# Cutting 12,160 tokens into 384 and 23 times 512, and loading a weight by one DMA for each 32 partitions

## The chip, the core and the metric

The kernel runs on one core of a Trainium2 chip. Its time is device time in microseconds (us) for one execution. Three runs of the kernel before took 2182.74, 2184.99 and 2193.29 us; the median, 2184.99 us, is the time before. The profile comes from one more execution, which took 2181.22 us. Its span, from the first instruction to the end of the last, is 2179.4 us; 1.8 us lie around it.

The engines are named as in the profile: PE multiplies matrices, DVE and ACT work on vectors, SP issues DMAs, and PEld is PE loading a stationary operand.

## The reference

Three stages over two sequences of 6080 tokens of width 256, in float32:

```
f = lower_bound + (1 - lower_bound) * sigmoid(f_logit);  h = f*h + (1-f)*x   # a scan over the tokens
y1 = relu(h @ w_in1)**2 @ w_out1                                             # 256 -> 2048 -> 256
y2 = elu(y1 @ w_in2) @ w_out2                                                # 256 -> 2048 -> 256
```

## The kernel before

**Tiling.** The 12,160 tokens are cut into blocks (`block_sizes`): one of 256, then 22 of 512, a rest of 384, and one of 256, 25 blocks in all. A slot is one block, one of the two layers (`m` = 0 or 1) and one of eight groups of 256 of the 2048 inner features. For each slot PE first makes the group's inner features in PSUM ("first" and "later"), ACT and DVE evict them and apply the activation, and PE then adds the group's share of the output to accumulators ("out"). After the eighth group ACT copies the accumulators out: layer 0 goes through DRAM and comes back as the input of layer 1, layer 1 goes to the result.

**Precision.** Each operand is held as a high and a low part of 32-bit numbers, and a product is three matmuls. All matmuls have a stationary operand of 128 x 128; what differs is the number of columns that move past it.

**Matmuls of a slot, for a block of n tokens.** The input product cuts the block into two halves and the features into two, and makes the four products of that 2 x 2 scheme by seven block products: 21 matmuls of n/2 columns (line 600). The first four blocks of layer 0 (`PLAIN = 4`) use eight block products instead, laid out as 12 matmuls of n columns (line 614). The output product of layer 0 is 12 matmuls of n columns (line 699, written as acc<-g,wo), that of layer 1 is 6n/128 matmuls of 256 columns (line 699, acc<-wo,g).

**Order over blocks.** Blocks are taken in pairs. A run is one layer over one pair, its slots woven together, the pair's second block starting two slots after its first. The runs are layer 0 of pairs 0 and 1, then in turn layer 1 of a pair and layer 0 of the pair two further on, and at the end layer 1 of the last two pairs. With 25 blocks the thirteenth pair holds one block, the last of 256 tokens, alone. Layer 1 of blocks 2 and 3 is the first run in which every block has 512 tokens and both layers' weights are made.

**Weights.** In the first run each of the eight groups of layer 0's input weights is loaded (`add_weights`, its step `load`), turned into its high and low part by two instructions of ACT (lines 371, 374) and four of DVE or ACT (377, 380, 397 or 399, 403), and stored to DRAM. Later runs stream the groups back in from DRAM (line 460), once for each run. `load_w` issues the load. For layer 0's input weights it is two DMAs on SP's queue, one for each half k of the 256 rows (line 320): each fills all 128 partitions, and its rows in DRAM are ordered as 4 groups q of 32 partitions i. Output weights are one DMA (line 313), layer 1's input weights one DMA (line 316).

**The scan.** `add_scan` loads half a block of `f_logit` and of `x` by four DMAs each (line 533, one for each 32 partitions), transposes them, applies the gate, and scans. The tiles `fs` and `xs` have one buffer each, so a half's loads wait until the half before has been transposed (line 542). `add_parts` then makes the high and low parts of the block, which PE reads (lines 492, 494, 500).

**What sets the order.** Every piece of work is a step with an engine, a cost and a due time. `Order.run` goes through the steps with these costs and writes out one list, by earliest due time among what is ready; each engine executes its part of the list in order. Before that list come a dummy activation of ACT (line 864), two DMAs of `lower_bound` on SP's queue (line 866), and two DVE instructions that make `ga` and `gb` from it (867, 868).

Of the kernel before, what the change touches and what calls it, by code (L numbers as in the profile page):

```python
# [11 lines left out]
AF = mybir.ActivationFunctionType  # L12
ALU = mybir.AluOpType
# [2 lines left out]
P = 128  # L16
TB = 512
HB = 256
FIRST = (256,)
LAST = (256,)  # L20
LEAD = 2
PLAIN = 4
BEHIND = 2
# [14 lines left out]
def block_sizes(total):  # L38

    ends = sum(FIRST) + sum(LAST)  # L40
    mid = [TB] * ((total - ends) // TB)
    rest = total - ends - sum(mid)
    return [*FIRST, *mid, *([rest] if rest else []), *LAST]

# [110 lines left out]
def kernel(  # L155
# [11 lines left out]
    nc = tc.nc  # L167
# [3 lines left out]
    KD = D // P  # L171
# [15 lines left out]
    lb = const.tile([P, KD], F32, name="lb")  # L187
    ga = const.tile([P, KD], F32, name="ga")
    gb = const.tile([P, KD], F32, name="gb")
    carry = const.tile([P, KD], F32, name="carry")  # L190
    warm = const.tile([P, 1], F32, name="warm")
# [41 lines left out]
    def new(tag, shape, dtype=F32, name=None):  # L233
        return pools[tag].tile(shape, dtype, tag=name or tag, name=name or tag)
# [29 lines left out]
    for i, s in enumerate(slots + [None] * (LAG + 1)):  # L264
        n = sizes[s[1]] if s else 0
        if s:
            if s[0] == 1 and s[2] == 0:
                while any(p[:2] == (0, s[1]) for _, p, _ in pending):
                    _, p, _ = pending.pop(0)
# [6 lines left out]
        while pending and (not s or i - pending[0][0] >= LAG or now - pending[0][2] >= AGE * sizes[pending[0][1][1]] / TB):  # L276
            _, p, _ = pending.pop(0)
# [9 lines left out]
    order = Order()  # L287

    def act(n, psum=False):
        return (0.05 if psum else 0.09) + n / 1172  # L290

    def dve(n, fast=False):
        return 0.067 + n / (1920 if fast else 960)

    def chain(due, steps):

        left = sum(st[1] + order.SLACK for st in steps)
        for e, us, what, *rest in steps:
            order.add(e, us, due - left, what, *rest)
            left -= us + order.SLACK  # L300
# [4 lines left out]
    CF = 256  # L305
    CE = 512
    ws_t = {}

    def load_w(st, m, kind, c):
        w = ((w_in1, w_out1), (w_in2, w_out2))[m][kind].bitcast(I32)  # L310
        if kind == 1:
            v = w[c * CF : (c + 1) * CF, :].rearrange("(k p) u -> p k u", p=P)
            nc.sync.dma_start(st.rearrange("p k e w -> p k (e w)"), v)
        elif m == 1:
            v = w[:, 2 * c * CF : 2 * (c + 1) * CF].rearrange("(k p) u -> p k u", p=P)
            nc.sync.dma_start(st.rearrange("p k e w -> p k (e w)"), v)
        else:
            v = w[:, 2 * c * CF : 2 * (c + 1) * CF].rearrange("(q k i) u -> k q i u", q=4, k=KD)
            for k in range(KD):
                nc.sync.dma_start(st[:, k].rearrange("p e w -> p (e w)"), v[k])  # L320

    n_a = {"a": 0, "wp": 0}

    def key_of(tag):
        n_a[tag] += 1
        return tag, n_a[tag] - 1
# [31 lines left out]
    def add_weights(i, m, kind, c, due, wk=None):  # L358
        t = {}

        def load(e):
            t["st"] = new("st", [P, 2, CE // 2, 2], I32)
            load_w(t["st"], m, kind, c)
            sv = t["st"].rearrange("p k e w -> p (k e) w")
            t["low"], t["high"] = sv[:, :, 0], sv[:, :, 1]

# [41 lines left out]
        def keep_whole(e):  # L408
            nc.sync.dma_start(rd[c], t["a"])

        st, a = ("st", i), key_of("a")
        steps = [
            ["SP", 0.95 if m == 0 and kind == 0 else 0.475, load, (), [st], None, 512],
            ["ACT", act(CE), scaled, [st], [a]],
            ["ACT", act(CE), low_bits, (), [st]],
            ["DVE", dve(CE), magnitude, [st], [a]],
            ["DVE", dve(CE), sign, [st], [a]],
        ]
        if m == 1 and kind == 0:
            q = key_of("a")  # L420
            chain(due - 6.0, [*steps, ["DVE", 4 * dve(P), sums, [a], [q]]])
            add_kept_parts(t, "a", a, m, c, 0, due - 2.0)
            add_kept_parts(t, "q", q, m, c, 4, due)
            return
        w = ("ws", wk) if kind == 0 else ("w", m, c)
# [96 lines left out]
    def add_scan(i, b, h, due):  # L522
        n = sizes[b] // 2
        t0 = starts[b] + h * n
        u = n_unit[0, b]
        t = {}
# [16 lines left out]
            return go  # L543

        def gate(e):
            f = t["fT"]
            for c in range(KD):
                nc.vector.tensor_scalar(f[:, c], f[:, c], ga[:, c : c + 1], gb[:, c : c + 1], op0=ALU.mult, op1=ALU.add)  # L548
# [274 lines left out]
    for due, what, m, g, s in weights:  # L823
        if what == "load":
            add_stream(m, s[1], g, due, n_ws)
        elif what == "sums":
            add_sums(g, due)
        else:
            add_weights(n_prep, m, int(what == "out"), g, due, n_ws)
            n_prep += 1  # L830
        if s:
            use[s] = n_ws
            n_ws += 1
# [6 lines left out]
    for kind, s in pe_order:  # L840
        m, b, g = s
# [19 lines left out]

    with tc.manual_schedule():
        nc.vector.memset(warm, 0.0)
        nc.scalar.activation(warm, warm, AF.Exp)
        for c in range(KD):
            nc.sync.dma_start(lb[:, c : c + 1], lower_bound.rearrange("(q c i o) -> c q i o", q=4, c=KD, o=1)[c])
        nc.vector.tensor_scalar(ga, lb, -0.5, 0.5, op0=ALU.mult, op1=ALU.add)
        nc.vector.tensor_scalar(gb, lb, 0.5, 0.5, op0=ALU.mult, op1=ALU.add)
        order.run()


# [23 lines left out]
```

## Time and profile before

| | us |
|---|---|
| time, median of 3 runs | 2184.99 |
| the profiled execution's own time | 2181.22 |
| its span | 2179.4 |
| PE busy | 2085.8 (96% of the span), 15072 matmuls |
| PE loading stationary operands | 1968.1 (90%) |
| DVE busy | 1729.9 (79%) |
| ACT busy | 1712.1 (79%) |
| mean granted clock of PE | 0.997 |
| DMA | 282.84 MB, 130 GB/s in the mean |

The share of busy time is a mean over stages with different limits. A matmul's busy time overlaps with that of the next one, since they are pipelined; what one matmul costs is read from the time between the starts of two neighbouring rows of the timeline, divided by the number of matmuls. A stretch of PE is read from where a run's first matmul starts: 25.8 us for the first of all, 379.4 us for layer 1 of blocks 2 and 3, and from there on one layer-1 run and one layer-0 run at a time.

### The profile page before, as it was taken

The numbers are of one execution on the slowest core, as the hardware profiler recorded it, in microseconds if no ns is written. First come the engines' busy times: TensorE is split into PE (matmuls) and PEld (weight loads), VectorE is DVE, ScalarE is ACT, GpSimd is POOL, SyncE is SP. The second block draws the span as 40 slices with busy tenths as digits, with TensorE's granted clock in tenths as the row PEclk, the third lists the DMA queues.
The fourth block names the chain that finished last, engine by engine and source line by source line (L and its number), as shares of the span: only waits on it lengthen the run. The fifth ranks groups of instructions, "written<-read, shape, count | busy, mean of one in ns | idle before, by whom it ended". The sixth has DMA issues, their size and how long they took to land.

```text
span 2179.4 us, 38016 instructions
## 1 busy us (share of the span) xinstructions
PE 2085.8 (96%) x15072; PEld 1968.1 (90%) x15072; DVE 1729.9 (79%) x2938; ACT 1712.1 (79%) x2243; POOL 0.2 (0%) x4
## 2 busy tenths in 40 slices
PE   2999899999999999999999999999999999999998
PEld 1877889999999899899899899999999989999998
DVE  5787896986985986987887798798698598677675
ACT  3786787887887887888888888788788788778675
POOL 0000000000000000000000000000000000000000
PEclk9999999999999999999999999999999999999999
DMA  5777643432542442433433433343253243233524
GB/s 154 218 236 241 194 157 108 120 124 94 135 130 95 130 130 92 133 101 119 120 109 124 126 102 124 113 115 126 100 136 122 95 123 127 87 112 106 185 85 141
DMA packets 213049, 282.84 MB, mean 130 GB/s; under 512 B 111112, under 2 KB 137608, under 8 KB 212872
## 3 DMA queue, kind: packets, MB, share of 16 engines
q1 hardware_dynamic: 212872, 280.42, 41.2%
q8 instruction: 119, 1.95, 0.4%
q14 instruction: 58, 0.48, 0.1%
HBM read 236.59 MB, written 43.78 MB: 129 GB/s over the span
## 4 chain that ended last, share of the span: by engine, by line
PE 68%; DVE 19%; ACT 6%; DMA 4%; issue 2%; SPq 1%; DVEq 0%; ACTq 0%
PE acc L699 35%; PE pc L600 31%; DVE g L672 4%; DVE r L643 2%; DVE F L565 2%; PE pc L614 1%; DVE r L662 1%; DVE s L631 1%; ACT s L628 1%; DVE r L639 1%; DMA ws<-wd 1%; DVE s L636 1%; DMA xs<-in_x_dram 1%; DVE fT L548 1%; DVE xA L500 1%
## 5 line engine op out<-in xcount | busy, mean ns | idle before, releaser
L699 PE MATMUL acc<-wo,g 128*128 128x256 f32 x4560 | 585.1, 283 | 17.8 <-DVE g L672 16.7
L699 PEld LDWEIGHTS acc<-wo,g 128*128 128x128 f32 x4560 | 561.3, 189 | 23.2 <-DVE g L672 21.4
L699 PE MATMUL acc<-g,wo 128*128 128x512 f32 (+2 forms) x2400 | 555.9, 382 | 2.1 <-DVE wo L403 2.1
L600 PE MATMUL pc<-xB,ws 128*128 128x256 f32 (+2 forms) x3864 | 507.6, 281 | 11.7 <-ACT s L628 11.2
L600 PE MATMUL pc<-xA,ws 128*128 128x256 f32 (+2 forms) x3864 | 506.3, 280 | 12.9 <-ACT s L628 12.9
L600 PEld LDWEIGHTS pc<-xA,ws 128*128 128x128 f32 x3864 | 481.6, 189 | 24.2 <-ACT s L628 18.5
L672 DVE TENSOR_TENSOR g<-r,g 128x1024 fp32r<-128x1024 f32 (+2 forms) x400 | 465.6, 1164 | 45.0 <-ACT g L667 43.9
L600 PEld LDWEIGHTS pc<-xB,ws 128*128 128x128 f32 x3864 | 482.5, 189 | 20.4 <-ACT s L628 13.7
L699 PEld LDWEIGHTS acc<-g,wo 128*128 128x128 f32 x2400 | 427.8, 189 | 78.0 <-DVE wo L403 2.3
L667 ACT ACTIVATE g<-r 128x1024 fp32r<-128x1024 f32 (+2 forms) x400 | 406.3, 1016 | 58.0 <-DVE r L662 50.6
L636 DVE TENSOR_TENSOR s<-pc,s 128x256 f32<-128x256 f32 (+2 forms) x368 | 150.5, 409 | 286.8 <-PE pc L600 286.1
L628 ACT ACTIVATE s<-pc 128x768 f32<-128x768 f32 (+2 forms) x368 | 286.9, 780 | 62.4 <-PE pc L600 61.1
L643 DVE TENSOR_TENSOR r<-pc,s 128x512 f32<-128x512 f32 (+2 forms) x368 | 244.3, 664 | 11.3 <-ACT r L646 5.9
L662 DVE SCALAR_TENSOR_TENSOR r<-e,r 128x1024 f32<-128x1024 f32 (+1 forms) x200 | 232.3, 1162 | 25.2 <-ACT e L659 25.2
L646 ACT ACTIVATE r<-pc 128x256 f32<-128x256 f32 (+2 forms) x368 | 137.0, 372 | 139.2 <-DVE r L643 87.1
L656 ACT ACTIVATE e<-r 128x1024 f32<-128x1024 f32 (+1 forms) x200 | 202.8, 1014 | 19.3 <-DVE r L639 14.9
L649 ACT ACTIVATE r<-r 128x768 f32<-128x768 f32 (+2 forms) x168 | 138.5, 824 | 97.8 <-DVE r L639 97.7
L652 ACT ACTIVATE r<-r 128x1024 f32<-128x1024 f32 (+1 forms) x200 | 203.6, 1019 | 5.7
L659 ACT ACTIVATE e<-e 128x1024 f32<-128x1024 f32 (+1 forms) x200 | 203.2, 1016 | 5.1
L631 DVE TENSOR_TENSOR s<-s 128x256 f32<-128x256 f32 (+2 forms) x368 | 150.1, 408 | 16.8 <-ACT s L628 9.4
L639 DVE TENSOR_TENSOR r<-s 128x256 f32<-128x256 f32 (+2 forms) x368 | 149.5, 406 | 0.0
L614 PE MATMUL pc<-xA,ws 128*128 128x256 f32 (+1 forms) x192 | 41.0, 368 | 29.0 <-DVE xA L494 25.8
(49 smaller groups left out, 858.0 us busy)
## 6 DMA issues: line engine op xcount, KB each, us to landing
ws<-wd SPq DMA_DIRECT2D x192, 896.0 KB
out_dram<-o SPq DMA_DIRECT2D x47, 256.0 KB
fs<-in_f_logit_dram SPq DMA_DIRECT2D x176, 64.0 KB
xs<-in_x_dram SPq DMA_DIRECT2D x176, 64.0 KB
xd<-o SPq DMA_DIRECT2D x44, 256.0 KB
F<-xd SPq DMA_DIRECT2D x44, 256.0 KB
st<-in_moe_w_out_dram SPq DMA_DIRECT2D x16, 512.0 KB
wd<-wp SPq DMA_DIRECT2D x24, 256.0 KB
```

What stands on the lines that cost most here:

```text
L600: nc.tensor.matmul(t["pc"][:, c], lhsT=ws[:, p, w], rhs=x_t[m, b][:, r, v], start=(which is FIRST_PRODUCTS and q == 0 and c in (1, 2)), st ...
L628: nc.scalar.activation(t["s"], t["pc"][:, 1:4], AF.Copy)
L631: nc.vector.tensor_tensor(t["s"][:, 1], t["s"][:, 1], t["s"][:, 2], op=ALU.add)
L636: nc.vector.tensor_tensor(t["s"][:, 0], t["pc"][:, 0], t["s"][:, 0], op=ALU.add)
L643: nc.vector.tensor_tensor(t["c"][:, 1:3], t["pc"][:, 2:4], u, op=ALU.add)
L652: nc.scalar.activation(t["r"], t["r"], AF.Square)
L656: nc.scalar.activation(t["e"], t["r"], AF.Relu, scale=-1.0)
L659: nc.scalar.activation(t["e"], t["e"], AF.Exp, scale=-1.0)
L662: nc.vector.scalar_tensor_tensor(t["r"], t["e"], 1.0, t["r"], op0=ALU.subtract, op1=ALU.max)
L667: nc.scalar.activation(t["g"][:, 0], t["r"], AF.Copy)
L672: nc.vector.tensor_tensor(t["g"][:, 1], t["r"], t["g"][:, 0].bitcast(F32), op=ALU.subtract)
L699: nc.tensor.matmul(a, lhsT=u, rhs=v, start=clear and k == 0, stop=two and k == 2, skip_group_check=True)
```

## The change

Five edits. `FIRST` and `LAST` make the blocks 384 and 23 times 512: 24 blocks, twelve full pairs. `load_w` takes the queue as an argument, and layer 0's input weights are loaded by four DMAs, one for each 32 partitions, each of them with both halves k; the step's cost in the plan goes from 0.95 to 1.9. The first of these loads is issued on ACT's queue, and its step is put ahead of all others (due -20, cost 0.1 on SP). Behind it on ACT's queue come the two DMAs of `lower_bound`, and then the dummy activation. `ga` and `gb` are made in the first `gate`.

```diff
-FIRST = (256,)
-LAST = (256,)
+FIRST = (384,)
+LAST = ()
...
-    def load_w(st, m, kind, c):
+    def load_w(queue, st, m, kind, c):
...
-            nc.sync.dma_start(st.rearrange("p k e w -> p k (e w)"), v)
+            queue.dma_start(st.rearrange("p k e w -> p k (e w)"), v)
...
-            v = w[:, 2 * c * CF : 2 * (c + 1) * CF].rearrange("(q k i) u -> k q i u", q=4, k=KD)
-            for k in range(KD):
-                nc.sync.dma_start(st[:, k].rearrange("p e w -> p (e w)"), v[k])
+            v = w[:, 2 * c * CF : 2 * (c + 1) * CF].rearrange("(q k i) u -> q i k u", q=4, k=KD)
+            for q in range(4):
+                queue.dma_start(st[32 * q : 32 * q + 32].rearrange("p k e w -> p k (e w)"), v[q])
...
-            load_w(t["st"], m, kind, c)
+            load_w(nc.scalar if i == 0 else nc.sync, t["st"], m, kind, c)
+            if i == 0:
+                for k in range(KD):
+                    nc.scalar.dma_start(lb[:, k : k + 1], lower_bound.rearrange("(q c i o) -> c q i o", q=4, c=KD, o=1)[k])
+                nc.scalar.activation(warm, warm, AF.Exp)
...
-            ["SP", 0.95 if m == 0 and kind == 0 else 0.475, load, (), [st], None, 512],
+            ["SP", 0.1 if i == 0 else 1.9 if m == 0 and kind == 0 else 0.475, load, (), [st], None, 512],
...
+        if i == 0:
+            order.add(*steps[0][:2], -20.0, *steps[0][2:])
+            del steps[0]
...
         def gate(e):
+            if i == 0:
+                nc.vector.tensor_scalar(ga, lb, -0.5, 0.5, op0=ALU.mult, op1=ALU.add)
+                nc.vector.tensor_scalar(gb, lb, 0.5, 0.5, op0=ALU.mult, op1=ALU.add)
...
     with tc.manual_schedule():
         nc.vector.memset(warm, 0.0)
-        nc.scalar.activation(warm, warm, AF.Exp)
-        for c in range(KD):
-            nc.sync.dma_start(lb[:, c : c + 1], lower_bound.rearrange("(q c i o) -> c q i o", q=4, c=KD, o=1)[c])
-        nc.vector.tensor_scalar(ga, lb, -0.5, 0.5, op0=ALU.mult, op1=ALU.add)
-        nc.vector.tensor_scalar(gb, lb, 0.5, 0.5, op0=ALU.mult, op1=ALU.add)
         order.run()
```

## Rows read from the trace of the kernel before

**Rows 1.** The page's first part: busy us, share of the span, instructions.

```profile
PE 2085.8 (96%) x15072; PEld 1968.1 (90%) x15072; DVE 1729.9 (79%) x2938; ACT 1712.1 (79%) x2243; POOL 0.2 (0%) x4
```

**Rows 2.** Busy time by stretch: stretch, its length, busy us of each engine, clock, DMA.

```profile
core 0: us, PE busy (x) PEld busy (x) DVE busy (x) ACT busy (x) POOL busy (x), PEclk, DMA share, GB/s
0.00:25.80 25.80, 0.00 (x0) 0.00 (x0) 9.65 (x27) 5.37 (x9) 0.20 (x4) 1.00 0.32 90
25.80:51.00 25.20, 9.20 (x37) 8.03 (x37) 19.68 (x37) 13.83 (x23) 0.00 (x0) 1.00 0.74 205
...
223.70:310.00 86.30, 76.54 (x625) 74.25 (x625) 81.22 (x160) 66.32 (x101) 0.00 (x0) 1.00 0.60 183
...
379.40:551.70 172.30, 170.12 (x1250) 161.49 (x1249) 141.24 (x232) 140.79 (x178) 0.00 (x0) 1.00 0.37 117
...
1585.60:1757.90 172.30, 170.12 (x1250) 161.48 (x1249) 141.27 (x232) 140.80 (x178) 0.00 (x0) 1.00 0.38 116
```

**Rows 3.** Timeline of PE late in the run: start us, us, instructions, idle before.

```profile
1758.96 2.91 PE L699 MATMUL acc<-g,wo 128*128 128x512 f32 x12
1761.71 2.63 PE L600 MATMUL pc<-xA,ws 128*128 128x256 f32 x21
...
1931.08 4.36 PE L699 MATMUL acc<-g,wo 128*128 128x384 f32 x24
1935.28 2.63 PE L600 MATMUL pc<-xA,ws 128*128 128x256 f32 x21
...
1944.35 2.73 PE L600 MATMUL pc<-xA,ws 128*128 128x256 f32 x12 [1.90 <-ACT s L628]
...
1951.34 1.59 PE L600 MATMUL pc<-xB,ws 128*128 128x256 f32 x12
1952.77 1.23 PE L600 MATMUL pc<-xA,ws 128*128 128x256 f32 x9
1953.84 3.04 PE L699 MATMUL acc<-wo,g 128*128 128x256 f32 x24
1956.72 1.58 PE L600 MATMUL pc<-xA,ws 128*128 128x256 f32 x12
...
2034.04 2.46 PE L600 MATMUL pc<-xA,ws 128*128 128x128 f32 x21
2036.33 1.64 PE L699 MATMUL acc<-g,wo 128*128 128x256 f32 x12
```

**Rows 4.** Timeline of SP's DMA issues at the start.

```profile
2.12 1.89 SPq L533 DMA_DIRECT2D fs<-in_f_logit_dram  x4
...
8.57 4.42 SPq L533 DMA_DIRECT2D fs<-in_f_logit_dram  x4
13.09 6.80 SPq L533 DMA_DIRECT2D xs<-in_x_dram  x4
```

**Rows 5.** Who waited for whom up to 130 us: us in total, times, longest.

```profile
ACT a L371 <- DMA st<-in_moe_w_in_dram: 26.7, 6, 8.3
```

**Rows 6.** Busy time in three short stretches, for the DMA share and rate at the end.

```profile
48.00:50.00 2.00, 0.00 (x0) 0.00 (x0) 0.98 (x4) 1.24 (x3) 0.00 (x0) 1.00 0.26 99
35.00:37.00 2.00, 1.33 (x6) 1.33 (x7) 2.00 (x6) 1.50 (x4) 0.00 (x0) 1.00 1.04 394
38.00:40.00 2.00, 0.17 (x1) 0.00 (x0) 1.97 (x5) 1.94 (x4) 0.00 (x0) 1.00 1.36 218
```

**Rows 7.** Timeline of PE and DVE at the very end.

```profile
2169.34 3.26 PE L699 MATMUL acc<-wo,g 128*128 128x256 f32 x24
...
2169.54 0.29 DVE L636 TENSOR_TENSOR s<-pc,s 128x128 f32<-128x128 f32 x1 [0.40 <-PE pc L600]
...
2174.16 1.46 PE L699 MATMUL acc<-wo,g 128*128 128x256 f32 x10 [0.23 <-DVE g L672]
```

**Rows 8.** Timeline of ACT at the start.

```profile
0.72 1.28 ACT L864 ACT_TABLE_LOAD   x1 [0.72 <-PEq L881]
...
5.49 0.42 ACT L537 ACTIVATE fs<-fs 128x256 f32<-128x256 f32 x1 [3.27 <-DMA fs<-in_f_logit_dram]
```

More of the change, by code (lines that the diff above doesn't have):

```diff
@@ L312, in load_w @@
             v = w[c * CF : (c + 1) * CF, :].rearrange("(k p) u -> p k u", p=P)
-            nc.sync.dma_start(st.rearrange("p k e w -> p k (e w)"), v)
+            queue.dma_start(st.rearrange("p k e w -> p k (e w)"), v)
         elif m == 1:
             v = w[:, 2 * c * CF : 2 * (c + 1) * CF].rearrange("(k p) u -> p k u", p=P)
-            nc.sync.dma_start(st.rearrange("p k e w -> p k (e w)"), v)
+            queue.dma_start(st.rearrange("p k e w -> p k (e w)"), v)
         else:
-            v = w[:, 2 * c * CF : 2 * (c + 1) * CF].rearrange("(q k i) u -> k q i u", q=4, k=KD)
-            for k in range(KD):
-                nc.sync.dma_start(st[:, k].rearrange("p e w -> p (e w)"), v[k])
+            v = w[:, 2 * c * CF : 2 * (c + 1) * CF].rearrange("(q k i) u -> q i k u", q=4, k=KD)
+            for q in range(4):
+                queue.dma_start(st[32 * q : 32 * q + 32].rearrange("p k e w -> p k (e w)"), v[q])
     n_a = {"a": 0, "wp": 0}
```

## The prediction, made before the changed kernel ran

> **What bounds the kernel now.** I read the page's busy times first, then busy time by stretch, then the timeline of PE, and last the start on all queues. PE is busy for 96% of the span, DVE and ACT for 79% [rows 1], so time is won by less PE work or by less waiting of PE. The stretches show where it waits [rows 2]. Up to 25.8 us PE does nothing, from there to 51.0 it works for 9.2 of 25.2 us, and from 223.7 to 310.0 for 76.5 of 86.3, beside a DVE busy for 81.2. From 379.4 us on a layer-1 run and a layer-0 run of 512-token blocks take 172.3 us together, of which PE waits 2.2; eight such periods follow each other, first and last shown. From 1757.9 to the end at 2179.4 come 421.5 us with the last blocks.
>
> PE's price for a matmul is the distance between starts [rows 3]. With 256 columns it is 119 ns (21 from 1951.34 to 1953.84) or 120 ns (24 to 1956.72). With 512 it is 229 ns (12 in 2.75 us), with 384 175 ns (24 in 4.20 us). But with 128 columns it is still 109 ns (21 from 2034.04 to 2036.33): a narrow matmul saves next to nothing. I take 110 for 192 columns, which must lie between 109 and 119. A 512-token slot of layer 1 costs 21 x 0.119 + 24 x 0.120 = 5.38 us.
>
> At the start the loads of layer 0's input weights are slow. SP issues a small load in 0.47 us (1.89 for four); the four at 8.57 take 4.42 us and the next four 6.80 [rows 4]. Up to 130 us ACT waits 26.7 us, in six waits, for these weights [rows 5]. When nothing but such a load runs, the DMA engines are busy for 0.26 and move 99 GB/s; when output weights run, for 1.04, at 394 GB/s; when loads of half blocks run, from 38 to 40 us, for 1.36 [rows 6]. So the old form uses a quarter of the 16 engines.
>
> **The change, part by part.** I add up the new time in the same three stretches.
>
> *End.* After the change there are nine periods from the first run of two 512-token layer-1 blocks (blocks 2 to 19 of layer 1, 6 to 23 of layer 0), then layer 1 of the last two pairs. Nine periods are 9 x 172.3 = 1550.7 us. What follows: 32 slots x 5.38 = 172.2; the last three output products of layer 0 before them, 36 x 0.229 = 8.2; 2.2 of waits in each run as in a period, 4.4; at the change from one layer-1 run to the next a wait like the 1.90 at 1944.35 [rows 3], 2. At the very end two output products cover the last slot's chain on DVE and ACT. Before, the chain took 4.6 us (2169.54 to 2174.16) against 24 matmuls from 2169.34, 2.9 us [rows 7]. At 512 tokens the cover is 5.8, the chain between 4.6 (no operation grows) and 9.2 (all double); the wait is 0 to 3.4, I take 2. From PE's last matmul to the end of the span 3.8 us passed (2174.16 + 1.46 to 2179.4); I keep that. Sum 192.6, bounds 190 and 203 (each second slot waiting 0.6 more). Together 1743.3 against 8 x 172.3 + 421.5 = 1799.9: 56.6 us less. Most of it is the narrow matmuls: 504 of 128 and 336 of 192 columns (168 for each layer of a block, the plain ones apart) become 168 of 192 and 336 more of 256. The rest is a short pair that waits more.
>
> *Start, PE's own work.* Block 0 grows by 128 tokens: 96 plain input matmuls from 119 to 175 ns, +5.4; 96 of its layer-0 output from 122 (as 256 columns elsewhere) to 175, +5.1; layer-1 output 48 matmuls more, +5.8; its layer-1 input 168 x 1 ns, +0.2. Sum 16.5. The first 2.0 (36 x 56 ns, the three slots ahead of block 1) lie inside the wait for block 1, so 14.5 are on the path.
>
> *Start, until block 1.* PE reaches block 1 at 51.0 us. If the loads spread over all engines, two things can bound this. SP: 32 loads of half blocks, twelve for weights 1 to 3 and some six others, 50 at 0.47, are 23.5 us from 0.7. Behind them come the landing, 1.5 us as from 4.0 to the tanh at 5.49 [rows 4, 8], and nine steps of DVE and ACT, an estimate of 0.7 us each like the widest steps around them: 32 us. DVE: 9.65 + 19.68 = 29.3 us of work before 51.0 [rows 2]. Block 0 is a third of the tokens, so at most a third of this, and grows by half, at most 4.9; weights are much of the rest, so I add 3. From 5.9 us, when the first tanh is done, that is 38.2 us without any wait. If the old chain keeps all but the first wait, it is 48. I take 40, the row of DVE with 2 us of waits: 11 us less, bounds 3 and 19.
>
> *Start, ACT's queue.* Six DMA issues stand ahead of the table load of 1.28 us and the first tanh, which began at 5.49 when its data came [rows 8]. No DMA is issued on ACT in this trace. The nearest rows are SP's: 0.47 free, 1.70 blocked [rows 4], so 2.8 to 10.2 us. I take 0.47, the row of an empty queue: 0.7 + 2.8 + 1.5 = 5.0, before the old 5.49. At the other end the first tanh is 7 us late, and with it everything up to block 1, unless DVE is late anyway; below nothing too, since SP loses two issues ahead of the first half. On DVE ga and gb (0.17 us each) now wait behind the transpose for the small DMAs, which are issued by 3.5 us and land with the first weights.
>
> *Start, after block 1.* The old form's waits that fall after 51 us go: 3 us, bounds 0 and 6. Later DVE is the limit (81.2 of 86.3 us [rows 2]). Block 0 in layer 1 brings it up to half more on eight slots, while the earlier start gives it room; I take nothing, bounds 8 either way. SP issues two more DMAs for each of seven weights, 14 x 0.47 = 6.6 us, beside PE work. If that cover is gone, they are in the 32 us above.
>
> So the first stretch is 379.4 + 0.5: -11 + 14.5 - 3 = +0.5.
>
> *Streams.* One run of each layer's weights less, 16 loads. The DMA share in a period is 0.38, so they were hidden: nothing.
>
> **Sum.** 379.9 + 1743.3 = 2123.2 us of span, with 1.8 around it 2125.0 against the profiled 2181.2. The median of the runs lies 3.8 above that execution, so I forecast 2126.
>
> **Rivals.**
> *The loads stay slow.* A DMA of 32 partitions might not use more engines than the old one. Then block 1 stays at 51.0, the 3 us stay, and three weights' additional issues (6 x 0.47) come on top: 2126 + 11 + 3 + 3 = 2143. Against it: four groups outermost and a quarter of the engines go together, and the loads of half blocks, themselves of 32 partitions, keep all engines busy [rows 6]. The Trainium skill (DMA: Bandwidth & Descriptors, Rules for kernel authors) speaks for this rival: transfers to separate parts of the partitions gain nothing, one transfer of all 128 should be used. The same section also says that an outermost dimension smaller than 16 confines a DMA to that many engines, which agrees with the 0.26 for four; by this second rule the new form, with 32 outermost, uses all of them.
> *SP is the bound.* DVE does less before block 1, since weights are turned later: block 1 at 32, 8 us less, 2118. For it speaks that DVE idles through most of the first 25.8 us; against it, that DVE works on output weights whenever scan data are late.
> *The end waits more.* Two layer-1 runs in a row wait as at 1944.35 in several places, each second slot of the last 16 some 0.9: 8 us, 2134.
> *Slower than before.* The plan is worked out anew for other block sizes, and the order may settle in a period with a wait of PE for its eviction in each slot. The nine periods have 288 slots, so it decides from 59/288 = 0.20 us a slot; at 0.25 the time is 2198. Against it: the pattern of two full pairs is the same, and eight periods agree within 0.1 us.
>
> **Chances.** Forecast 0.60, loads stay slow 0.10, SP the bound 0.15, the end waits more 0.10, slower order 0.05. The forecast's own bounds are 19 below and 22 above: 2107 to 2148, which takes in the first three rivals. By a measurement 0.5%, 11 us, can be told from no change. All cases but the last are faster by more than that, and of the last I give 0.01 to no change: faster 0.95, same 0.01, slower 0.04.
>
> **What would show it right or wrong.** Right: 15072 - 336 - 96 = 14640 matmuls (two input products and one layer-0 output product of a block fewer), nine periods of 172.3 us, PE's first matmul near 15 us (20 issues at 0.47 up to the second half's loads, from 0.7, landing 1.5, then six short steps of about 0.5), block 1's near 40, a DMA share near 1 in the loads of layer 0's weights, no wait of ACT for them beyond the first. Wrong: a period that is longer, which would cost nine times; a first layer-1 run of full blocks that begins after 390 us; or more than 203 us behind the ninth period.

## The result, and the profile after

The changed kernel takes 2114.14 us (median of 4 runs, 2113.18 to 2115.37), the kernel before 2183.86 beside it (4 runs): ratio 0.9675, 95% interval 0.965 to 0.970. Ratios here and below are of undisturbed runs, not of the two medians; two runs far off, one of 9898.39 us with the short block at the end and one of 2566.45 us of the kernel before beside it, are left out of them. The forecast was 2126, with 2107 to 2148 as its range. The profiled execution took 2113.18 us with a span of 2111.4, 68.0 less than the span before. The page's first part answers to [rows 1]:

```profile
PE 2041.2 (97%) x14640; PEld 1925.7 (91%) x14640; DVE 1717.8 (81%) x2833; ACT 1692.7 (80%) x2146; POOL 0.2 (0%) x4
```

PE has the 14640 matmuls of the forecast and 44.6 us less busy time; the other 23.4 us of the span are PE's idle time. Busy time by stretch, answering to [rows 2]:

```profile
core 0: us, PE busy (x) PEld busy (x) DVE busy (x) ACT busy (x) POOL busy (x), PEclk, DMA share, GB/s
0.00:22.95 22.95, 0.00 (x1) 0.03 (x1) 13.49 (x31) 9.22 (x16) 0.20 (x4) 1.00 0.75 178
22.95:43.10 20.15, 9.13 (x36) 8.40 (x36) 17.86 (x31) 12.86 (x19) 0.00 (x0) 0.80 0.89 275
...
43.10:373.90 330.80, 319.89 (x1897) 285.41 (x1898) 276.79 (x495) 256.54 (x340) 0.00 (x0) 0.99 0.61 187
...
223.70:310.00 86.30, 78.36 (x633) 75.87 (x632) 83.88 (x153) 66.91 (x92) 0.00 (x0) 1.00 0.49 149
373.90:546.20 172.30, 170.11 (x1250) 161.45 (x1249) 141.27 (x232) 140.95 (x178) 0.00 (x0) 1.00 0.37 117
...
1924.80:2111.40 186.60, 181.02 (x1478) 178.66 (x1476) 143.89 (x211) 146.42 (x181) 0.00 (x0) 1.00 0.26 88
```

From these rows and [rows 2] the 68.0 us divide as follows: until block 1 begins 43.1 instead of 51.0 us (-7.9); from there to the first period 330.8 instead of 328.4 (+2.4); nine periods and what follows them 1737.5 instead of eight periods and 421.5, 1799.9 (-62.4). PE's timeline has the limits of these stretches, and the changes of run and the end, answering to [rows 3, 7]:

```profile
22.95 0.66 PE L625 MATMUL pc<-xA,ws 128*128 128x384 f32 x1 [22.95 <-DVE xA L502]
...
43.12 0.80 PE L625 MATMUL pc<-xB,ws 128*128 128x512 f32 x1 [10.79 <-ACT xB L500]
45.29 4.45 PE L625 MATMUL pc<-xB,ws 128*128 128x512 f32 x11 [1.37 <-DVE xB L508]
...
373.89 1.22 PE L611 MATMUL pc<-xA,ws 128*128 128x256 f32 x9
...
1924.76 1.22 PE L611 MATMUL pc<-xA,ws 128*128 128x256 f32 x9
...
1940.40 1.22 PE L611 MATMUL pc<-xB,ws 128*128 128x256 f32 x9
...
2024.88 1.59 PE L611 MATMUL pc<-xA,ws 128*128 128x256 f32 x12
...
2103.45 0.51 PE L710 MATMUL acc<-wo,g 128*128 128x256 f32 x2 [0.28 <-ACT g L678]
2104.71 2.89 PE L710 MATMUL acc<-wo,g 128*128 128x256 f32 x22 [0.75 <-DVE g L683]
```

A row without brackets began with no wait: neither the entry into the last runs (1940.40) nor the change between them (2024.88) has the 1.90 us of [rows 3]. Behind 1924.76 PE waits only at the very end, 0.75 us at 2100.28 and in the two rows shown last, 1.8 in all. The nine periods are 1924.76 - 373.89 = 1550.9 us.

The start on the queues and engines, answering to [rows 4, 8]; q behind an engine's name is its issuing queue:

```profile
0.73 3.34 ACTq L321 DMA_DIRECT2D st<-in_moe_w_in_dram  x4
2.62 3.93 SPq L541 DMA_DIRECT2D xs<-in_x_dram  x4
4.82 1.71 ACTq L367 DMA_DIRECT2D lb<-in_lower_bound_dram  x2
6.56 1.28 ACT L368 ACT_TABLE_LOAD   x1 [6.56 <-DMA st<-in_moe_w_in_dram]
6.59 4.04 SPq L321 DMA_DIRECT2D st<-in_moe_w_in_dram  x8
...
9.05 0.51 ACT L545 ACTIVATE fs<-fs 128x384 f32<-128x384 f32 x1
9.18 0.69 DVE L382 SCALAR_TENSOR_TENSOR a<-a,st 128x512 int32<-128x512 int32 x1 [8.32 <-ACT st L379]
```

Four issues on ACT take 0.84 us each. The first tanh begins at 9.05 instead of 5.49, although its data had come (5.74, from the first row of the chain below). But eight loads of layer 0's weights now take 4.04 us to issue, 0.51 each; in the kernel before, four loads of a half block issued behind the old weight loads took 4.42 and then 6.80 us. ACT's waits up to 130 us, answering to [rows 5] (us, times, longest), and a stretch with hardly anything but new loads, answering to [rows 6]:

```profile
ACT a L376 <- DMA st<-in_moe_w_in_dram: 2.0, 3, 0.8
```

```profile
8.50:11.00 2.50, 0.00 (x0) 0.00 (x0) 1.82 (x4) 1.05 (x3) 0.00 (x0) 1.00 0.93 252
```

The wait fell from 26.7 to 2.0 us, the DMA share rose from 0.26 to 0.93.

What sets block 1 now? The chain that ended last, followed back and shown in order of time (start, us, what), goes through the two staging buffers of half blocks, of which there is one each (fs, xs):

```profile
1.66 4.08 DMA fs<-in_f_logit_dram
...
9.80 0.14 DVE xT L550
...
11.68 2.92 DMA fs<-in_f_logit_dram
...
17.80 0.49 DVE xT L550
...
26.12 0.69 DVE xT L550
...
31.84 5.00 DMA st<-in_moe_w_out_dram
36.84 0.69 DVE xT L550
```

DVE transposes a half block at 9.8, 17.8, 26.1 and 36.8 us: the buffer comes free with each transpose, the next load is issued behind it on SP, and the following transpose comes 8 to 11 us later. Not all of that is the round trip through the buffer: in between the chain also names DVE's work on weights and the load of an output weight (5.00 us at 31.84).

### The profile page after: what moved, and what is told of

It is laid out like the page before. It is cut to its first block, busy times and chain, and to the rows that moved or that the text cites. A ratio compares the mean times of both kernels' runs of the same rounds, so it can differ in the third digit from the quotient of the medians.

```text
span 2111.4 us, 36876 instructions
## 1 busy us (share of the span) xinstructions
PE 2041.2 (97%) x14640; PEld 1925.7 (91%) x14640; DVE 1717.8 (81%) x2833; ACT 1692.7 (80%) x2146; POOL 0.2 (0%) x4
## 4 chain that ended last, share of the span: by engine, by line
PE 71%; DVE 20%; ACT 4%; DMA 2%; issue 2%; SPq 1%; DVEq 0%; ACTq 0%
PE acc L710 38%; PE pc L611 30%; DVE g L683 4%; PE pc L625 4%; DVE r L654 2%; DVE F L576 2%; DVE r L673 2%; DVE s L642 1%; DVE r L650 1%; DVE s L647 1%; DVE fT L559 1%; DMA xs<-in_x_dram 1%; DVE fT L550 1%; DVE xA L508 1%; DVE xT L562 1%
## 5 line engine op out<-in xcount | busy, mean ns | idle before, releaser
L710 PE MATMUL acc<-g,wo 128*128 128x512 f32 (+1 forms) x2304 | 552.2, 389 | 0.0
L611 PE MATMUL pc<-xA,ws 128*128 128x256 f32 (+1 forms) x3696 | 486.1, 280 | 7.1 <-ACT s L639 7.1
L683 DVE TENSOR_TENSOR g<-r,g 128x1024 fp32r<-128x1024 f32 (+1 forms) x384 | 463.6, 1207 | 35.4 <-ACT g L678 34.3
L611 PE MATMUL pc<-xB,ws 128*128 128x256 f32 x3696 | 487.0, 281 | 3.9 <-ACT s L639 3.9
L678 ACT ACTIVATE g<-r 128x1024 fp32r<-128x1024 f32 (+1 forms) x384 | 403.1, 1050 | 58.3 <-DVE r L673 51.5
L647 DVE TENSOR_TENSOR s<-pc,s 128x256 f32<-128x256 f32 (+1 forms) x352 | 147.7, 420 | 283.5 <-PE pc L611 283.3
L639 ACT ACTIVATE s<-pc 128x768 f32<-128x768 f32 (+1 forms) x352 | 283.1, 804 | 48.8 <-PE pc L611 48.0
L654 DVE TENSOR_TENSOR r<-pc,s 128x512 f32<-128x512 f32 (+1 forms) x352 | 241.0, 685 | 7.7 <-ACT r L657 2.6
L642 DVE TENSOR_TENSOR s<-s 128x256 f32<-128x256 f32 (+1 forms) x352 | 147.4, 419 | 9.3 <-ACT s L639 0.7
L650 DVE TENSOR_TENSOR r<-s 128x256 f32<-128x256 f32 (+1 forms) x352 | 147.0, 418 | 0.0
```

The source lines that it names most:

```text
L611: nc.tensor.matmul(t["pc"][:, c], lhsT=ws[:, p, w], rhs=x_t[m, b][:, r, v], start=(which is FIRST_PRODUCTS and q == 0 and c in (1, 2)), st ...
L639: nc.scalar.activation(t["s"], t["pc"][:, 1:4], AF.Copy)
L642: nc.vector.tensor_tensor(t["s"][:, 1], t["s"][:, 1], t["s"][:, 2], op=ALU.add)
L647: nc.vector.tensor_tensor(t["s"][:, 0], t["pc"][:, 0], t["s"][:, 0], op=ALU.add)
L654: nc.vector.tensor_tensor(t["c"][:, 1:3], t["pc"][:, 2:4], u, op=ALU.add)
L678: nc.scalar.activation(t["g"][:, 0], t["r"], AF.Copy)
```

## The change taken apart

**Blocks alone.** The kernel before, with the new block sizes and nothing else:

```diff
-FIRST = (256,)
-LAST = (256,)
+FIRST = (384,)
+LAST = ()
```

> The kernel before with only the blocks changed, to 384 and 23 times 512. Theory (blocks and loads add up): the end as in the changed kernel, nine periods of 172.3 and 186.6 us, against 1799.9 before, so 62.4 less; the start loses what the loads gave, so layer 1 of blocks 2 and 3 begins at 379.4 plus 14.5, some 394 us, against 373.9 in the changed kernel: 2131 to 2136 us. Rival 1 (the loads are worth nothing, the whole gain is from the blocks): 2114. Rival 2 (at the end the waits come from the plan that the loads' new costs gave, not from the blocks): the last part is 192 us or more and the time is over 2138.

Measured: 2129.6 us (2129.43 to 2129.73) against 2183.83, ratio 0.9757 (0.9742 to 0.9771): 54.2 us of the 69.7 (1.4 us below the range of its theory). Its PE timeline, ACT's wait and the stretch from block 1 to the first period (columns as above):

```profile
53.98 0.79 PE L614 MATMUL pc<-xB,ws 128*128 128x512 f32 x1 [10.67 <-ACT xB L492]
```

```profile
ACT a L371 <- DMA st<-in_moe_w_in_dram: 25.6, 6, 8.7
```

```profile
54.00:390.20 336.20, 322.43 (x1897) 285.81 (x1898) 277.84 (x494) 258.65 (x346) 0.00 (x0) 0.99 0.60 187
```

The old loads wait as before, block 1 comes 3.0 us later behind a larger block 0, and from there the way to the first period is 7.8 us longer, not 14.5. The end is that of the changed kernel: 1737.6 us from the first period on, against 1737.5.

**Loads alone.** The changed kernel with the old block sizes:

```diff
-FIRST = (384,)
-LAST = ()
+FIRST = (256,)
+LAST = (256,)
```

> The changed kernel with the blocks of before (256, 22 times 512, 384, 256); loads, queue and costs as changed. Theory: block 1 is reached near 41 us instead of 51, and of the waits behind it (8 us in layer 0 of blocks 2 and 3, with two stretches of half clock) most go: 12 to 20 us less than before, 2164 to 2172 us, the end unchanged at about 421 us from the ninth layer-1 run on. Rival 1 (the loads only matter together with a larger first block): 2180 or more. Rival 2 (the waits behind block 1 went because of the larger first block): about 10 us less, 2174.

Measured: 2176.11 us (2174.37 to 2179.84), ratio 0.9973 (0.9962 to 0.9984): only 7.7 us less, between what its two rivals said. The two edits together give 69.7, so on the new blocks the loads are worth 15.5. PE reaches block 1 at 42.35, but the first period only at 375.2. Its stretches, and those of the kernel before that answer to them:

```profile
42.30:375.20 332.90, 315.60 (x1849) 279.77 (x1850) 264.42 (x488) 247.50 (x342) 0.00 (x0) 0.96 0.60 185
232.50:249.60 17.10, 15.35 (x70) 15.06 (x71) 12.29 (x25) 6.75 (x11) 0.00 (x0) 0.50 0.42 131
```

```profile
51.00:379.40 328.40, 311.92 (x1849) 274.39 (x1850) 263.16 (x485) 251.43 (x349) 0.00 (x0) 0.98 0.61 192
...
91.20:94.60 3.40, 3.40 (x10) 2.63 (x10) 2.17 (x3) 3.31 (x6) 0.00 (x0) 0.50 0.94 306
```

PE's timeline of the kernel before at the second of these rows, and at the next stretch like it, which begins at 135.5 (a third begins at 214.1):

```profile
89.83 1.46 PE L699 MATMUL acc<-g,wo 128*128 128x256 f32 x10 [2.06 <-DVE wo L403]
91.13 4.50 PE L614 MATMUL pc<-xB,ws 128*128 128x512 f32 x12
95.47 1.59 PE L614 MATMUL pc<-xA,ws 128*128 128x256 f32 x12
...
135.99 4.15 PE L614 MATMUL pc<-xB,ws 128*128 128x512 f32 x11 [1.48 <-DVE xB L500]
139.98 2.28 PE L614 MATMUL pc<-xA,ws 128*128 128x512 f32 x9
```

Of the 8.7 us won at block 1, 4.5 are given back behind it: for the same 1849 matmuls PE is busy 3.7 us longer and idle 0.8 longer. In the profiled execution the busy time goes into a stretch of 17.1 us in which TensorE was granted its lower clock, 1.2 GHz (0.50 in the PEclk column). The kernel before has three such stretches of 3.4 us: there twelve 512-column matmuls take 4.34 us from start to start of the next, 362 ns each instead of 229. The changed kernel has none after 48.9 us (its row 43.10:373.90 has 0.99 in that column). Nor have the blocks alone, with the old loads, after 60 us (0.99 or 1.00), so they went with the block sizes and not with the loads, though how was not tested; with the larger first block the gain is kept. The mean granted clock of a whole run points the same way, 0.989 to 0.991 in all seven runs of the loads alone, 0.996 or 0.997 in the four of the changed kernel.

**The form of the loads.** The changed kernel with each weight loaded by two DMAs of 128 partitions again, four groups outermost; all else as changed:

```diff
-            v = w[:, 2 * c * CF : 2 * (c + 1) * CF].rearrange("(q k i) u -> q i k u", q=4, k=KD)
-            for q in range(4):
-                queue.dma_start(st[32 * q : 32 * q + 32].rearrange("p k e w -> p k (e w)"), v[q])
+            v = w[:, 2 * c * CF : 2 * (c + 1) * CF].rearrange("(q k i) u -> k q i u", q=4, k=KD)
+            for k in range(KD):
+                queue.dma_start(st[:, k].rearrange("p e w -> p (e w)"), v[k])
```

> The changed kernel, but layer 0's input weights again by two DMAs of 128 partitions, one for each half of the rows; first load, small DMAs and dummy activation on ACT's queue and all costs of the plan as changed, so the order of work is the same. Theory (the old form runs on a quarter of the DMA engines): a DMA share of about 0.25 while they run, ACT waits for these weights again for 15 us or more in total, block 1 is reached at 48 to 56 us instead of 43, and the time is 5 to 14 us above the changed kernel's 2114. Rival (the gain is from the first load being early on its own queue, not from the form): block 1 within 2 us of 43 and the time within 2 us of 2114.

Measured: 2132.77 us (2130.5 to 2133.36), ratio 0.9772 (0.9756 to 0.9789): 18.6 more than the changed kernel, above what was expected.

```profile
54.10 0.80 PE L625 MATMUL pc<-xB,ws 128*128 128x512 f32 x1 [12.41 <-ACT xB L500]
```

```profile
ACT a L376 <- DMA st<-in_moe_w_in_dram: 30.1, 9, 5.8
```

ACT waits 30.1 us again and block 1 comes 11.0 us later. While nothing but such loads runs, from 56 to 60 us, the DMA share is 0.26 again. The form is all of the loads' gain: with the old form, what else the edit moves buys nothing, for this kernel is 3.2 us slower than the blocks alone.

**ACT's queue.** The first weight and the bounds issued at the head of SP's queue, the table load first on ACT again:

```diff
-            load_w(nc.scalar if i == 0 else nc.sync, t["st"], m, kind, c)
+            load_w(nc.sync, t["st"], m, kind, c)
...
-                    nc.scalar.dma_start(lb[:, k : k + 1], lower_bound.rearrange("(q c i o) -> c q i o", q=4, c=KD, o=1)[k])
-                nc.scalar.activation(warm, warm, AF.Exp)
+                    nc.sync.dma_start(lb[:, k : k + 1], lower_bound.rearrange("(q c i o) -> c q i o", q=4, c=KD, o=1)[k])
...
+        nc.scalar.activation(warm, warm, AF.Exp)
```

> The changed kernel, but the first load and the two small DMAs stand at the head of SP's queue and the dummy activation is ACT's first instruction again; form and plan as changed. Theory A (ACT's queue costs: its six issues took 0.84 us each and the table load began at 6.56, the first tanh at 9.05 us): without them the first weight is turned from about 4.5 us and the first tanh is at about 6.5, DVE starts 2.5 us earlier, block 1 is reached at 40 to 42 instead of 43.1, the time is 1 to 3 us below 2114. Theory B (SP's issues bound the start): six more issues of 0.47 on SP ahead of the first half's loads make everything 2.8 us later, block 1 at 45 to 46, the time 2 to 3 us above 2114.

Measured: 2112.92 us (2112.46 to 2113.98), ratio 0.9681 (0.9667 to 0.9695): no difference from the changed kernel that can be told. PE, ACT and what DVE waited for up to 44 us:

```profile
5.37 0.66 ACT L375 ACTIVATE a<-st 128x512 f32<-128x512 f32 x1 [3.15 <-DMA st<-in_moe_w_in_dram]
...
7.50 0.52 ACT L544 ACTIVATE fs<-fs 128x384 f32<-128x384 f32 x1 [0.94 <-DMA fs<-in_f_logit_dram]
...
43.12 0.80 PE L624 MATMUL pc<-xB,ws 128*128 128x512 f32 x1 [11.04 <-ACT xB L499]
```

```profile
DVE xT L549 <- DMA xs<-in_x_dram: 2.7, 1, 2.7
```

ACT begins on the weight at 5.37 instead of 7.96, but DVE then waits for xs, which SP now issues from 5.91 instead of 2.62 on, and block 1 begins at 43.12 in both. Neither a gain nor a loss expected of the queue came. The tanh comes 1.5 us earlier and is not on the path, as xs comes no earlier.

**What the form does.** The same loads split in eight, 32 partitions and half of k each, so that the outermost dimension stays 32 and the number of issues doubles:

```diff
-                queue.dma_start(st[32 * q : 32 * q + 32].rearrange("p k e w -> p k (e w)"), v[q])
+                for k in range(KD):
+                    queue.dma_start(st[32 * q : 32 * q + 32, k].rearrange("p e w -> p (e w)"), v[q, k])
```

> The changed kernel, but each of layer 0's input weights loaded by eight DMAs, one for each 32 partitions and each half of the rows; queue and plan as changed. It has the new form's outermost dimension (32 partitions) and the old form's separate halves. Theory (what counts is the outermost dimension, four groups before, 32 now): the DMA engines stay at a share near 0.9 while these loads run, ACT waits little for them; SP issues four DMAs more for each weight, 1.9 us, three times before block 1, so block 1 comes 0 to 6 us later than 43.1 and the time is 2114 to 2121 us. Rival (the halves k in separate DMAs are what made the old form slow): like the run with the old form, ACT waits some 30 us for these weights, block 1 at 54, 2132 us.

Measured: 2117.16 us (2116.36 to 2117.55; before 2181.7), ratio 0.968 (0.9639 to 0.9722). In its PE timeline block 1 stands at 45.17, 2.1 later, not near 54; while it loads, the DMA share is half, not the 0.9 expected. Issuing now limits it: 16 issues of 64 KB take 7.29 us, which makes some 140 GB/s, an estimate that meets the rate of the row.

```profile
45.17 0.80 PE L626 MATMUL pc<-xB,ws 128*128 128x512 f32 x1 [10.83 <-ACT xB L501]
```

```profile
8.00:11.00 3.00, 0.00 (x0) 0.00 (x0) 1.90 (x4) 1.47 (x3) 0.00 (x0) 1.00 0.49 140
```

So the separate halves are not what made the old form slow. Nor, it seems, that its DMAs fill all 128 partitions and are few: an output weight is one such DMA, and with two of them on the way, beside other transfers, the share is 1.04 [rows 6]. What both fast forms have and the old one lacks is a large outermost dimension, 32 against 4; the additional issues cost 3 us.

## The start, tested further

**Short block at the end.** 23 blocks of 512, then 384:

```diff
-FIRST = (384,)
-LAST = ()
+FIRST = ()
+LAST = (384,)
```

> The changed kernel with the odd block at the end: 23 times 512 and then 384. PE's own work grows by 17.9 us at the start and falls by 14.0 at the end. Theory (a short block beside a long one makes PE wait, as in the kernel before, where the period with 512 and 384 tokens took 172.1 us though it has 6.7 us less work): the first period begins near 393 us, the period with the short block is about 172 us, what follows the last period 178 to 186 us: 2124 to 2132 us. Rival (only PE's own work counts): 2114 + 3.9 - 2 hidden behind the wait for block 1, 2114 to 2117 us.

Measured: 2117.06 to 2119.22 us, ratio 0.9681 (0.9615 to 0.9748), between what the sides expected. Its stretch:

```profile
43.10:381.60 338.50, 334.63 (x1944) 294.12 (x1945) 287.09 (x498) 267.40 (x343) 0.00 (x0) 0.99 0.59 184
```

PE has 14.7 us more to do behind block 1 (334.63 against 319.89), but arrives only 7.7 later: its idle time fell from 10.9 to 3.9. From 223.7 to 310.0 DVE is as busy as in the changed kernel (82.85 against 83.88 us) and PE is busy for 84.75 instead of 78.36: with two full blocks in the first pair there is more PE work to do while DVE is the limit. A wait ahead of 192-column matmuls is back at the end (0.74 us at 2097.85).

**DVE's load before block 1.** The gate of the first two blocks on ACT instead of DVE:

```diff
-                nc.vector.tensor_scalar(f[:, c], f[:, c], ga[:, c : c + 1], gb[:, c : c + 1], op0=ALU.mult, op1=ALU.add)
+                if b < 2:
+                    nc.scalar.activation(f[:, c], f[:, c], AF.Identity, bias=gb[:, c : c + 1], scale=ga[:, c : c + 1])
+                else:
+                    nc.vector.tensor_scalar(f[:, c], f[:, c], ga[:, c : c + 1], gb[:, c : c + 1], op0=ALU.mult, op1=ALU.add)
```

> The changed kernel, but the gate of the first two blocks' four half blocks (two DVE instructions each, 0.33 to 0.37 us each) is computed by ACT with the same numbers; the order of work stays. Theory (up to block 1 DVE is the bound: busy 12.65 of 13.0 us from 10 to 23 and 17.7 of 20 from 23 to 43): 2.8 us less on DVE, block 1 at 40 to 42, time 2111 to 2113. Rival (the DMAs of block 1 or SP's issues bound it): block 1 within 0.5 us of 43.1, time 2114; or later, if ACT's place in the chain costs more than DVE saves.

Measured: 2114.36 us (2113.84 to 2114.59), ratio 0.9668 (0.9626 to 0.9709), block 1 at 43.62. From 23 to 43 us:

```profile
23.00:43.00 20.00, 8.93 (x36) 8.24 (x36) 16.43 (x27) 14.21 (x23) 0.00 (x0) 0.80 0.88 265
```

```profile
DVE xT L565 <- ACT fT L560: 1.9, 1, 1.9
```

DVE was relieved (17.71 us in this stretch of the changed kernel) and nothing came of it. But it now waits 1.9 us for the gate on ACT, more than the 1.3 that it was relieved of, so this run does not settle whether its load is the bound.

**Output weights later.** The due time of the first run's output weights moved by 8 us:

```diff
-        weights.append((out_due[0, 0, g], "out", 0, g, None))
+        weights.append((out_due[0, 0, g] + 8.0, "out", 0, g, None))
```

> The changed kernel, but the first run's output weights are due 8 us later in the plan, so that on DVE some seven of their instructions move from ahead of block 1's scan to behind it. Theory (block 1 waits for DVE's queue of weight work that isn't needed yet): block 1 at 36 to 40 us instead of 43.1, and since DVE has room behind it (74.7 of 79 us busy up to 130), most of it is kept: 2109 to 2113 us. Rival (the same DVE work is due anyway): block 1 earlier, but PE waits for output weights in the next slots, the first period begins again at 374 us, 2114.

Measured: 2117.52 us (2116.05 to 2118.33), ratio 0.9682 (0.964 to 0.9723).

```profile
41.80:376.80 335.00, 323.35 (x1897) 287.62 (x1898) 278.73 (x497) 260.81 (x349) 0.00 (x0) 0.98 0.59 186
```

Block 1 comes 1.3 us earlier, and the way behind it takes 4.2 more, so that the kernel ends slower than either side said. Of the 4.2, 3.5 are PE's busy time; up to 130 us PE waits only 0.5 us for an output weight. The lead is gone by 60 us (18.2 us with 68 matmuls, where the changed kernel takes 16.9 with 69); where the rest goes was not tested.

**Two staging buffers.** The chain above points to fs and xs. A second buffer of each, with the room for it taken from a and wp; beside it a control that gives up the same room and has one of each:

```diff
-    "fs": 1, "xs": 1, "fT": 1, "xT": 1, "F": 2, "xA": 1, "xB": 1, "ws": 4, "wp": 3, "r": 3, "e": 1,
-    "g": 3, "s": 2, "st": 3, "a": 5, "o": 2, "pc": 2, "acc": 4,
+    "fs": 2, "xs": 2, "fT": 1, "xT": 1, "F": 2, "xA": 1, "xB": 1, "ws": 4, "wp": 2, "r": 3, "e": 1,
+    "g": 3, "s": 2, "st": 3, "a": 4, "o": 2, "pc": 2, "acc": 4,
```

> The changed kernel with two buffers instead of one for each of the tiles fs and xs, and, to make room, four instead of five of a and two instead of three of wp (both of the weights' making). Theory (up to block 1 the bound is the round trip through the one buffer: issue 3.8 us, landing, tanh, the transposes that free it, some 9 us a half block, four times): the next half's loads no longer wait for the transposes, PE begins at 17 to 20 us instead of 22.9 and reaches block 1 at 34 to 39 instead of 43.1; 3 to 8 us less than the control with the same smaller a and wp. Rival (DVE is the bound, 95% busy from 10 to 43 us): block 1 not before 41, within 2 us of the control.

The control's edit:

```diff
-    "fs": 1, "xs": 1, "fT": 1, "xT": 1, "F": 2, "xA": 1, "xB": 1, "ws": 4, "wp": 3, "r": 3, "e": 1,
-    "g": 3, "s": 2, "st": 3, "a": 5, "o": 2, "pc": 2, "acc": 4,
+    "fs": 1, "xs": 1, "fT": 1, "xT": 1, "F": 2, "xA": 1, "xB": 1, "ws": 4, "wp": 2, "r": 3, "e": 1,
+    "g": 3, "s": 2, "st": 3, "a": 4, "o": 2, "pc": 2, "acc": 4,
```

> The control: the changed kernel with four of a and two of wp, one of fs and xs as changed. Theory: weights are made with less room, all of it before 310 us: block 1 near 43, the first period begins 0 to 5 us later than 373.9, 2114 to 2119 us. Rival (the making of weights was bound by these buffers): 2120 or more.

Measured: 2110.74 us with two buffers (2109.49 to 2111.38, ratio 0.9662, 0.9636 to 0.9689), 2114.4 for the control (2114.09 to 2115.28, ratio 0.968, 0.9654 to 0.9707); before 2184.17. PE with two buffers:

```profile
33.12 6.10 PE L625 MATMUL pc<-xA,ws 128*128 128x384 f32 x24 [8.16 <-DVE ws L404]
39.06 2.96 PE L625 MATMUL pc<-xB,ws 128*128 128x512 f32 x12
```

PE's first matmul comes at 18.92 and block 1 at 39.06, without a wait and 3.9 us before the control's 42.91: the single buffers were the bound. What is late next are weights, for which PE waits 8.16 us ahead of it. The order of DVE's work changes with the buffers: block 1's halves are transposed from 18.2 and 23.3 us on instead of 26.1 and 36.8, and much of the weights' work moves behind them. In the changed kernel DVE is busy with both for 31.2 of the 34 us from 9 to 43; a test that keeps its order and adds the buffers alone was not made.

**The short block second.** 512, 384, then 22 of 512:

```diff
-FIRST = (384,)
+FIRST = (512, 384)
```

> The changed kernel with the odd block second: 512, 384 and 22 times 512. PE's own work is the same; both blocks are of the plain kind in layer 0, so only the first layer-1 run has narrow matmuls. Theory A (in that run DVE sets the pace, as the waits of 12.9 us with 384 and 512 against 3.2 with 512 and 512 show, and what stands in it doesn't depend on which block is short): the first period begins at 372 to 376 us, 2112 to 2116 us. Theory B (a short block that comes first makes the slots' starts come too soon for the evictions): waits of 3 to 7 us in that run, the first period begins at 364 to 370 us, 2105 to 2111 us. Block 1, shorter by a quarter, is reached at 40 to 43 us in both.

Measured: 2109.03 us (2107.84 to 2110.12), ratio 0.9657 (0.9625 to 0.9688), beside the same runs of the kernel before as the control.

```profile
40.70:368.10 327.40, 317.94 (x1896) 285.64 (x1897) 275.58 (x494) 255.69 (x347) 0.00 (x0) 0.99 0.61 190
```

Block 1, now of 384, begins 2.4 us earlier, and the way behind it is 3.4 shorter with the same matmuls to within one record. The time and the first period are those of theory B, its waits are not: behind block 1 they fell only from 10.9 to 9.5, and 2.0 of the 3.4 are PE's busy time; why that fell is open. It also shows that a first block of 512 alone does not bring the idle time of 3.9 above; that took a first pair of two.

**Both.** The last two edits together:

```diff
-FIRST = (384,)
+FIRST = (512, 384)
...
-    "fs": 1, "xs": 1, "fT": 1, "xT": 1, "F": 2, "xA": 1, "xB": 1, "ws": 4, "wp": 3, "r": 3, "e": 1,
-    "g": 3, "s": 2, "st": 3, "a": 5, "o": 2, "pc": 2, "acc": 4,
+    "fs": 2, "xs": 2, "fT": 1, "xT": 1, "F": 2, "xA": 1, "xB": 1, "ws": 4, "wp": 2, "r": 3, "e": 1,
+    "g": 3, "s": 2, "st": 3, "a": 4, "o": 2, "pc": 2, "acc": 4,
```

> The two edits that each were faster, together: blocks 512, 384 and 22 times 512, two buffers for each of fs and xs, four of a and two of wp. Theory (they act in different places, the buffers before block 1, the order of the two blocks mostly in the first layer-1 run, whose waits fell from 12.9 to 9.6): 2114.1 - 5.1 - 3.7 = 2105.3, between 2103 and 2108 us. Rival (both only shorten the same wait for block 1, which took 10.8 us in the changed kernel and 6.8 with the odd block second): 2108 to 2111 us, no better than the odd block second alone.

Measured: 2106.77 us (6 runs, 2105.05 to 2107.67) against 2185.36, ratio 0.9634 (0.961 to 0.9658). That is 7.4 of the 8.8 us that the two won apart (5.1 and 3.7), and in the range of the theory, not of the rival. No run of it is as slow as the fastest of the changed kernel or of the short block second, though they were not timed side by side. Its first period begins at 367.33, only 0.8 us before that of the short block second alone, where the second buffers alone brought 4.4 against the control (370.97 and 375.36): up to there the two edits win mostly the same time. The medians and this reading do not agree on how far the gains add up, and it stays open.

## Why the prediction came out as it did

The sum was right in its mechanism: fewer narrow matmuls at the end, whole engines for the loads at the start. It came out 12 us too high, 6 in the first stretch (379.9 said, 373.9 measured) and 6 in the last. In the first stretch two misses of opposite sign, 3.1 us too little until block 1 and 9.1 too much behind it, cancel in part; that much is luck. Two steps of the arithmetic do not follow: the stated bounds add up to 21.6 below and 29.4 above, ACT's queue apart, not 19 and 22; and with the 3.8 us named, 2125.0 gives 2129, not 2126 (measured, the median lies 1.0 above the profiled execution).

- *Nine periods:* 1550.7 said, 1550.9 measured, and 14640 matmuls as said. The rival of a slower order is out.
- *The end's gain:* from the first period on some 62 us were won, 52.5 in PE's busy time and 10 in its waits. Most of it is the narrow matmuls as said, some 34 us at the prices of [rows 3], an estimate; 110 ns for 192 columns was right (12 take 1.31 us at 2082.51 of the run with the short block at the end). But the rest is not only a short pair that waits more: some 12 us, estimated at the same prices, are output products of the 128 tokens that moved to block 0.
- *Behind the ninth period:* 192.6 said, 186.6 measured. The 4.4 us of waits in the two runs and the 2 at the change were mis-sized: they did not come (1940.40 and 2024.88 without a wait). I had carried them over from periods in which DVE also scans for new blocks; at the end it is busy for 143.89 of 186.60 us and has time. The ninth period's trace fits this, though no run tests it: its two waits for DVE, 0.61 us at 1776.40 and 1.02 at 1783.02, stand where DVE scans from 1769.7 to 1781.7 with no idle time. The rival that the end waits more is out by the 1.8 us measured. The 2 us for the very end were right: these are the 1.8.
- *Block 1:* 40 said, 43.1 measured. That the loads stop to bound was right (2.0 us of waits). DVE's work was sized right, 32.3 us said and 31.35 measured, but it began at 9.18 instead of 5.9. The step that failed is the path: the sum has SP's issues and DVE's load as the two things that can bound, and leaves out the round trip through one buffer of fs and one of xs. Moving six issues between queues changed nothing; the second buffers brought block 1 to 39.06. Relieving DVE was not a clean test, and no other run tests its load. PE's first matmul was said at 15 and came at 22.95: the sum issues the second half's loads straight behind the first's, but with one buffer they wait for its transposes and are issued from 10.84 on, and the first tanh came 3.6 us later. The second of each buffer takes 4 us off.
- *Behind block 1:* +14.5 for PE's work and -3 for waits, +11.5 said, +2.4 measured. PE's busy time grew by 8.0 (311.92 to 319.89) and its idle time fell by 5.6 (16.5 to 10.9). In the growth, three stretches at 1.2 GHz that the kernel before had (91.2, 135.5, 214.1 us) are gone; in the first two, at 12 matmuls from 91.13 to 95.47 and 11 from 135.99 to 139.98, against 0.229 each they cost 1.6 and 1.5 us, so some 4.5 for the three, an estimate from these two. The remaining 2 us are open. In the idle time, more PE work in the first pair fills what DVE had left open: with two blocks of 512 it is 3.9. The blocks alone give +7.8 there, and the new form against the old takes 336.6 (54.10 to 390.7) down to 330.8. I had put the effect of the DVE-paced stretch at nothing, with 8 either way.
- *ACT's queue:* 0.47 an issue said, 0.84 measured, inside its bounds of 0.47 to 1.70; the price is real (table load at 6.56, tanh at 9.05) and off the path.
- *The loads stay slow:* out. With the old form the DMA share was 0.26, in the kernel before [rows 6] and in the run that goes back to it, with the new one 0.93, and going back costs 18.6 us. Of the two rules of the Trainium skill weighed there (DMA: Bandwidth & Descriptors, Rules for kernel authors), the one that an outermost dimension under 16 confines a DMA to that many engines agrees with the runs; the one against transfers to separate partitions does not hold for this load, whose old form kept the DMA engines only 0.26 busy.

## What to carry to other kernels

Price a matmul by the distance of starts at each width before cutting blocks: here 128 columns cost 109 ns and 256 cost 119, and taking the narrow ones out won some 34 of the 62 us from the first period on. Look at the DMA share in a stretch with one kind of load alone; if it is a fraction, look at which dimension stands outermost before adding queues. When a wait at the start goes, follow the chain again: what came next was a single staging buffer, which no list of busy engines names. And test two gains together before adding them.

## What the hardware showed that was not expected

- Issues can be slower with two queues at work: 0.84 us on ACT, and 0.98 on SP for its second four (3.93 us; its first four beside ACT took 0.46), where SP alone took 0.45 to 0.48 for the same loads. The 14 issues of the changed kernel's two queues end at 6.55, those of SP alone at 7.80. The Trainium skill (DMA: Bandwidth & Descriptors, Rules for kernel authors) says that spreading over issuers gives no bandwidth and saves issue time only; here it saved 1.25 us of 14 issues, and none on the path.
- Granted clock: TensorE fell to 1.2 GHz in the middle of the work, after waits of 2.06 us (ahead of 91.2) and of 0.74 and 1.48 us (ahead of 135.5) in the kernel before, with 362 ns for a 512-column matmul instead of 229. In the loads alone a stretch at that level lasted 17.1 us. Behind the 1.90 us of 1944.35, too, the granted clock is 0.58 from 1944 to 1948. That the waits bring it about was not tested; if so, a wait costs more than its length.
- A granted clock of 1.00 in the profile does not prove the full pace: the kernel before has 1.00 from 51 to 57 us, where eleven 512-column matmuls take 405 ns each (53.07 to 57.53), as slow as in the changed kernel at 0.50 (389 ns, 45.29 to 49.57).
